# Two groups of DMA issues moved from ScalarE's queue to SyncE's in a fused attention and MoE kernel

## Chip, cores and metric

The kernel runs on one core of a Trainium2 chip. The metric is the device time of one launch in microseconds, from the first to the last instruction and what lies around it; lower is better. Times are medians of several runs.

## What is computed

The reference, cut to what matters:

```python
def _attn_ref(q, k, v, mem_k, mem_v):          # B=4, H=8, S=768, D=64
    chunk, left_ctx, right_ctx = (32, 16, 8)   # and 8 memory rows per head
    for c in range(S // chunk):
        k_full = concat([mem_k, k[l_start:r_end]]); v_full = concat([mem_v, v[l_start:r_end]])
        a = softmax(q_c @ k_full.T / sqrt(D))
        out[c] = a @ v_full
x = out.transpose(0, 2, 1, 3).reshape(3072, 512)
x = (sigmoid(x @ w_gate) * (x @ w_val)) @ w_out            # moe: 512 -> 1536 -> 512
h = x @ w_in; y = (h * sigmoid(1.702 * h)) @ w_out2        # moe2: 512 -> 2048 -> 512
```

All tensors are float32. The kernel keeps that precision by splitting each value into a high and a low fp32r part and multiplying three times.

## The kernel before

**Tokens.** The 3072 tokens are six blocks of 512 (`BLK`, `NB`). Attention works on 32 tiles of 96 tokens, each with all eight heads. Nine tiles go first; the other 23, called the late tiles here, are written by `attention_b` (L1001) in a fixed walk, one after the other, while TensorE works through the matmuls of moe for the first blocks (its input products L821 and L828, its output product L1020 in `gemm2`). The last two blocks' moe, and all of moe2, run later in a scheme of seven products in place of eight (L1318 and L1655); for these two blocks the attention's result goes through DRAM (`x_dram`).

**One late tile** in `attention` (L390): loads of q (12 DMAs into a buffer `f`), of k (16 to 20 DMAs into `raw` for a pair of tiles) and, for some, of mem_k; on VectorE the transposes `qt` (L532) and `kt` (L540), with copies of `kt` on ScalarE (L544); on TensorE one burst that holds the product with the values of the tile before (L704, `pv` from here on) and this tile's scores (L555); the softmax on VectorE, ScalarE and GpSimd; then `rest()` (L675), which loads the values, normalises, and transposes the probabilities. `rest()` calls `load_ctx("vn", ...)` (L405), which issues one DMA for v, one for mem_v and, at a sequence's first or last tile, one more. There is one buffer `vn`, so the loads for a tile can start when the tile before has had its `pv`, and have to land before its own. `evict()` (L720) copies the result out of PSUM: for the last two blocks on ScalarE into `qt` (L733), from where a DMA stores it to `x_dram`.

**What sets the order.** Every operation is a task with an engine, a planned duration, what it reads and writes, and for some a due time. `Schedule.run()` (L73) plays all tasks through in planned time and emits them, engine by engine, in the order in which they began there. On the chip every engine works its list in that order. A DMA's issue is a task of the engine that issues it. The helper `dma()` (L344) chooses it:

```python
q_ = nc.gpsimd if pool else nc.scalar if act else nc.sync
add("pool" if pool else "act" if act else "sp", dur, lambda: q_.dma_start(...), ...)
```

So ScalarE (ACT) issues what has `act=True`: before the change the late tiles' values and the stores to `x_dram`. It also issues the stores of moe's output to `y_dram` (L1044, with its own `nc.scalar.dma_start`). SyncE (SP) issues the loads of q, k and mem_k, the weights' loads, and everything of the later stages but a few.

**After the walk** `x_prep` (L1187) loads the four pieces of x of two blocks from `x_dram` on SP (L1194), forms their sums and differences (L1200) and high and low parts (L1178, L1182), and the seven products of L1318 begin. `produce1` (L1304) reloads weights from `wf_dram` for them.

Of the kernel before, what the change touches and what calls it, by code (L numbers as in the profile page):

```python
# [132 lines left out]
def c_dve(n, k=1):  # L133
    return k * 0.13 + n / 960.0


def c_act(n):
    return 0.13 + n / 1200.0
# [7 lines left out]
def kernel(  # L146
# [198 lines left out]
    def dma(dst, src, key, r=(), act=False, dur=0.45, pool=False):  # L345
        n = 8
        for d in src.shape:
            n *= d
        q_ = nc.gpsimd if pool else nc.scalar if act else nc.sync
        add("pool" if pool else "act" if act else "sp", dur, lambda: q_.dma_start(out=dst(), in_=src), r=list(r), w=[key], nbytes=n)  # L350
# [39 lines left out]
    def attention(t, bufs, banks, pe_path, extra=None, nth=0, last=False):  # L390
# [11 lines left out]
        def tadd(eng, dur, fn, r=(), w=(), more=0.0, **kw):  # L402
            add(eng, dur, fn, r=r, w=w, slack=SL + more, **kw)

        def load_ctx(name, src, mem, act=False):  # L405

            s0 = j * TQ - LEFT
            r0 = LEFT if j == 0 else 0
            r1 = TK - RIGHT if j == TPB - 1 else TK
            parts = [(r0, r1, src[b, :, s0 + r0 : s0 + r1, :]), (TK, P, mem[b])]  # L410
            if j == 0:
                parts.append((0, LEFT, src[b, :, 0:LEFT, :]))
            if j == TPB - 1:
                parts.append((r1, TK, src[b, :, S - RIGHT : S, :]))
            ks = []
            for i, (a, z, s) in enumerate(parts):
                ks.append((kk[name], i))
                dma(lambda a=a, z=z: T[name][a:z], s.rearrange("h s d -> s h d"), ks[-1], r=pre, act=act)
            for i in range(len(parts), 4):
                ks.append((kk[name], i))  # L420
            return ks
# [197 lines left out]
        def norm(eng, dst, rows_, keys):  # L619
            r = slice(*rows_)  # L620
            c = slice(*keys)
            n = rows_[1] - rows_[0]
            eng.tensor_tensor(  # L623
                out=dst, in0=e3()[r, :, c], in1=T["sm"][r].to_broadcast([n, H, keys[1] - keys[0]]), op=ALU.mult
            )

        if pe_path:

            def ev_norm(c):
                r = (c * CH, (c + 1) * CH)  # L630
                eng = nc.vector if en[c] == "dve" else nc.gpsimd
                norm(eng, T["pw"][r[0] : r[1], :, c * CH : c * CH + CTX], r, (0, CTX))

            def ev_norm_m():
                norm(nc.vector if en[0] == "dve" else nc.gpsimd, T["pw"][:, :, TK:P], (0, TQ), (CTX, KW))

            en = ["pool", "pool", "pool"] if t in (0, 2) else ["dve", "pool", "pool"]
            for c in range(NCK):
                tadd(en[c], 0.75 if en[c] == "dve" else 1.2, lambda c=c: ev_norm(c), r=ke + [kk["sm"]], w=[(kk["pw"], c)])
            tadd(en[0], 0.25 if en[0] == "dve" else 0.35, ev_norm_m, r=ke + [kk["sm"]], w=[(kk["pw"], 3)])  # L640

            def pe_pt(n):
                for h in range(H):
                    a, p = divmod(h, NP)
                    nc.tensor.transpose(  # L645
                        bt[a][:, p * TQ : p * TQ + n], T["pw"][:n, h, :], ident()[:n, :n]
                    )

            def ev_pt(a, n):
                src = bt[a][:, : NP * TQ].rearrange("p (h s) -> p h s", s=TQ)[:, :, :n]  # L650
                dst = T["pt"].rearrange("p (a h) s -> p a h s", a=2)[:, a, :, :n]
                nc.scalar.activation(dst, src, AF.Copy)

            def probs(n, more=()):
                bands = range(4) if n == TQ else (0, 3)
                r = [(kk["pw"], c) for c in bands] + [bufs.kid, *more]
                tadd("pe", 0.7 if n == TQ else 0.45, lambda: pe_pt(n), r=r, w=kbt, margin=mg)
                for a in range(2):
                    tadd("act", c_act(NP * n), lambda a=a: ev_pt(a, n), r=[kbt[a]], w=[(kk["pt"], a)])
        else:  # L660

            def ev_norm():
                norm(nc.gpsimd, T["pn"][0:L, :, 3 * CH - NM : 3 * CH], (0, L), (CTX, KW))
                norm(nc.gpsimd, T["pn"][L:TQ, :, CTX:KW], (L, TQ), (CTX, KW))

            PTB = ((0, 0, 0), (1, 0, 1), (2, 0, 2), (0, 1, 1), (1, 1, 2), (2, 1, 3), (0, 2, 3), (1, 2, 3))

            def ev_pt(part):
                for c, kb, r in PTB[2 * part : 2 * part + 2]:
                    nc.vector.transpose(  # L670
                        T["pt"][r * CH : (r + 1) * CH, :, c * CH : (c + 1) * CH],
                        T["pn"][c * CH : (c + 1) * CH, :, kb * CH : (kb + 1) * CH],
                    )

            def rest():  # L675
                load_ctx("vn", v, mem_v, True)
                tadd(
                    "pool",
                    0.95,
                    lambda: norm(nc.gpsimd, T["pn"][:, :, 0:CTX], (0, TQ), (0, CTX)),  # L680
                    r=ke + [kk["sm"]],
                    w=[(kk["pn"], 0)],
                )
                tadd("pool", 0.6, ev_norm, r=ke + [kk["sm"]], w=[(kk["pn"], 1)])
                for part in range(4):
                    tadd(
                        "dve",
                        0.88,
                        lambda part=part: ev_pt(part),
                        r=[(kk["pn"], 0), (kk["pn"], 1)],  # L690
                        w=[(kk["pt"], part)],
                    )
# [21 lines left out]
        def values(a, m, bk):  # L714
            if pe_path:
                return bk[:, : NP * TQ].rearrange("p (a s) -> p a s", a=NP)[:, :, a : a + m]
            src = both[:, :, NP * KW : NP * KW + NP // 2 * TQ]
            return src.rearrange("p o (a s) -> p o a s", s=TQ)[:, :, :, a : a + m]

        def evict(part=None, bk=bv, kpv=kpv):  # L720

            g = range(t * NCK, (t + 1) * NCK)
            for i, blk in enumerate(sorted({c // NCH for c in g})):
                if part not in (None, i):
                    continue
                cs = [c for c in g if c // NCH == blk]
                a = (cs[0] - g[0]) * CH
                m = len(cs) * CH
                x0 = cs[0] % NCH * CH
                xb = blk % 2  # L730
                if blk >= NB - 2:
                    src, dst = values(a, m, bk), T["qt"][:, :, :m].rearrange("p (o a) s -> p o a s", o=2)
                    tadd("act", c_act(NP * m), lambda d=dst, s=src: nc.scalar.activation(d, s, AF.Copy), r=kpv, w=[kk["qt"]])  # L733
                    o = (blk - NB + 2) * BLK + x0
                    dma(
                        lambda o=o, m=m: x_dram.rearrange("(a p) c -> p a c", p=P)[:, :, o : o + m],
                        T["qt"][:, :, :m],
                        ("xd", blk, t),
                        r=[kk["qt"]],
                        act=True,  # L740
                    )
                    continue
                due = None
                if t < NPRO and blk == 0:
                    due = clock[0] - STEP * (NPRO - 1 - t) - AHEAD
                elif t < NPE and blk <= 1 and SPREAD:

                    due = clock[0] + SPREAD * (t - NPRO + 1) / (NPE - NPRO)
                src = values(a, m, bk)
                wx = [("x", xb, c % NCH, e) for c in cs for e in range(2)]  # L750
                rx = kpv + (["x1"] if xb else [])

                def at(xs, x0=x0, m=m, xb=xb):
                    dst = xs[xb][:, :, x0 : x0 + m]
                    return dst if pe_path else dst.rearrange("p (o a) s -> p o a s", o=2)

                def ev_xh(src=src, at=at):
                    nc.scalar.activation(at(xhs), src, AF.Copy)

                def ev_xl(src=src, at=at):  # L760
                    nc.vector.tensor_tensor(out=at(xls), in0=src, in1=at(xhs).bitcast(F32), op=ALU.subtract)

                tadd("act", c_act(NP * m), ev_xh, r=rx, w=wx)
                tadd("dve", c_dve(NP * m), ev_xl, r=rx, w=wx, due=due)
# [1135 lines left out]
```

## Time and profile before

| | |
|---|---|
| median of 3 runs | 1128.76 us (1127.51 to 1131.07) |
| the profiled execution | 1130.38 us, span 1128.6 us |
| granted TensorE clock | 0.999 |
| TensorE matmul busy | 1116.4 us (99%) |
| VectorE, ScalarE, GpSimd busy | 842.4 us (75%), 589.6 us (52%), 161.6 us (14%) |
| DMA engines' mean busy share in the 40 slices | 0.2 to 0.9 |

The profile's page gives the busy time of each engine, in which the issuing of DMAs is not counted. The timeline lists what an engine did and, in brackets, how long it sat idle before and what ended that; a queue of an engine is written with a q (ACTq, SPq). The list of waits sums these idle times by pair of waiting and awaited line. The chain is the work that ended last, followed back from the end.

### The profile page before, as it was taken

The numbers are of one execution on the slowest core, as the hardware profiler recorded it, in microseconds if no ns is written. First come the engines' busy times: TensorE is split into PE (matmuls) and PEld (weight loads), VectorE is DVE, ScalarE is ACT, GpSimd is POOL, SyncE is SP. The second block draws the span as 40 slices with busy tenths as digits, with TensorE's granted clock in tenths as the row PEclk, the third lists the DMA queues.
The fourth block names the chain that finished last, engine by engine and source line by source line (L and its number), as shares of the span: only waits on it lengthen the run. The fifth ranks groups of instructions, "written<-read, shape, count | busy, mean of one in ns | idle before, by whom it ended". The sixth has DMA issues, their size and how long they took to land.

```text
span 1128.6 us, 19515 instructions
## 1 busy us (share of the span) xinstructions
PE 1116.4 (99%) x7190; PEld 933.7 (83%) x7190; DVE 842.4 (75%) x1440; ACT 589.6 (52%) x972; POOL 161.6 (14%) x209
## 2 busy tenths in 40 slices
PE   7999999999999999999999999999999999999998
PEld 6888899997888888888888888888888888888886
DVE  7989746776767788888887788869966369575365
ACT  5888632222222344676666777666455365354452
POOL 4332244122333113200001110000000000000000
PEclk9999999999999999999999999999999999999999
DMA  9676344335433555542556867868796666776526
GB/s 208 203 216 196 90 122 114 52 67 119 102 83 79 150 145 174 199 161 104 177 178 245 305 216 269 271 244 295 245 255 211 200 203 219 233 216 204 170 86 176
DMA packets 245903, 203.13 MB, mean 180 GB/s; under 512 B 170928, under 2 KB 191920, under 8 KB 245808
## 3 DMA queue, kind: packets, MB, share of 16 engines
q1 hardware_dynamic: 201560, 162.29, 48.9%
q0 software_dynamic: 6880, 24.12, 5.7%
q10 hardware_dynamic: 37368, 15.47, 5.0%
q8 instruction: 57, 0.93, 0.3%
q14 instruction: 38, 0.31, 0.1%
HBM read 151.49 MB, written 50.33 MB: 179 GB/s over the span
## 4 chain that ended last, share of the span: by engine, by line
PE 97%; DMA 1%; SPq 1%; ACT 0%; DVE 0%; issue 0%; ACTq 0%
PE bank L1318 30%; PE bank L1655 20%; PE bank L1020 18%; PE bank L821 15%; PE bank L828 8%; PE both L704 2%; PE both L555 2%; SPq L350 1%; PE bank L704 1%; PE bank L885 0%; DMA kn<-in_mem_k_dram 0%; PE bank L645 0%; DMA vn<-in_v_dram 0%; DMA w<-wo_dram 0%; PE both L645 0%
## 5 line engine op out<-in xcount | busy, mean ns | idle before, releaser
L1318 PE MATMUL bank<-sb_x,sb_r 128*128 128x512 f32 x1512 | 347.4, 389 | 0.0
L1318 PEld LDWEIGHTS bank<-sb_x,sb_r 128*128 128x128 f32 x1512 | 283.8, 188 | 58.9
L1655 PE MATMUL bank<-wq,w 128*128 128x512 f32 x756 | 178.0, 389 | 0.4 <-DMA w<-wo_dram 0.4
L1655 PEld LDWEIGHTS bank<-wq,w 128*128 128x128 f32 x756 | 141.8, 188 | 30.3 <-issue 0.8
L821 PE MATMUL bank<-xh,w 128*128 128x512 f32 (+1 forms) x464 | 159.6, 355 | 0.0
L821 PE MATMUL bank<-xl,w 128*128 128x512 f32 (+1 forms) x464 | 158.6, 353 | 0.0
L1334 DVE TENSOR_TENSOR sb_s<-bank,sb_s 128x512 f32<-128x512 f32 x108 | 74.4, 690 | 83.0 <-PE bank L1318 75.8
L828 PE MATMUL bank<-xh,w 128*128 128x512 f32 (+1 forms) x464 | 108.8, 356 | 0.0
L1020 PE MATMUL bank<-gh,wq 128*128 128x512 f32 (+1 forms) x448 | 98.7, 360 | 0.0
L821 PEld LDWEIGHTS bank<-xh,w 128*128 128x128 f32 x464 | 87.8, 189 | 12.6
L821 PEld LDWEIGHTS bank<-xl,w 128*128 128x128 f32 x464 | 87.8, 189 | 11.9
L1330 ACT ACTIVATE sb_s<-bank 128x512 f32<-128x512 f32 x108 | 64.8, 604 | 50.7 <-PE bank L1318 49.9
L828 PEld LDWEIGHTS bank<-xh,w 128*128 128x128 f32 x464 | 78.1, 189 | 12.4
L1020 PEld LDWEIGHTS bank<-gh,wq 128*128 128x128 f32 x448 | 76.4, 189 | 12.9
L670 DVE STREAM_TRANSPOSE pt<-raw 32x256 f32<-32x256 f32 x184 | 79.5, 432 | 4.7 <-POOL raw L623 2.1
L1626 DVE TENSOR_TENSOR wq<-xh_g,wq 128x1024 fp32r<-128x1024 f32 (+1 forms) x60 | 60.5, 1008 | 22.9 <-ACT wq L1623 22.5
L1623 ACT ACTIVATE wq<-xh_g 128x1024 fp32r<-128x1024 f32 (+1 forms) x60 | 53.3, 889 | 35.2 <-PE bank L1655 34.2
L853 ACT ACTIVATE gh<-sig 128x512 fp32r<-128x512 f32 (+1 forms) x58 | 32.3, 557 | 67.4 <-DVE sig L848 61.6
L623 POOL TENSOR_TENSOR raw<-e,sm 96x448 f32<-96x448 f32 (+2 forms) x69 | 41.0, 606 | 176.1 <-DVE sm L615 149.0
L1655 PE MATMUL bank<-wq,w_e 128*128 128x512 f32 x252 | 62.5, 389 | 0.0
L845 ACT ACTIVATE sig<-bank 128x512 f32<-128x512 f32 (+1 forms) x58 | 30.5, 526 | 55.5 <-PE bank L828 49.7
L1655 PEld LDWEIGHTS bank<-wq,w_e 128*128 128x128 f32 x252 | 47.3, 188 | 9.8
(215 smaller groups left out, 1646.1 us busy)
## 6 DMA issues: line engine op xcount, KB each, us to landing
sb_r<-wc_dram SPq DMA_DIRECT2D x133, 256.0 KB
w<-wo_dram SPq DMA_DIRECT2D x63, 512.0 KB
w_e<-wo_dram SPq DMA_DIRECT2D x21, 512.0 KB
wc_dram<-sb_r SPq DMA_DIRECT2D x15, 512.0 KB
wo_dram<-w POOLq DMA_DIRECT2D x14, 512.0 KB, 3.9
raw<-in_moe_w_out_dram SPq DMA_DIRECT2D x13, 512.0 KB
raw<-in_moe_w_in_dram SPq DMA_DIRECT2D x13, 512.0 KB
wf_dram<-f POOLq DMA_DIRECT2D x24, 256.0 KB, 2.9
```

The costliest lines, as they stand in the source:

```text
L623: eng.tensor_tensor(out=dst, in0=e3()[r, :, c], in1=T["sm"][r].to_broadcast([n, H, keys[1] - keys[0]]), op=ALU.mult)
L670: nc.vector.transpose(T["pt"][r * CH : (r + 1) * CH, :, c * CH : (c + 1) * CH], T["pn"][c * CH : (c + 1) * CH, :, kb * CH : (kb + 1) * CH],)
L704: nc.tensor.matmul((bk if to is None else to)[hp * D : (hp + 1) * D, o : o + q], T["vn"][:, 2 * p + hp, :], T["pt"][:, hp * NP + p, :q], s ...
L821: nc.tensor.matmul(bank[bk][:, :n], w[:, 0, ts[t]], x[xb][:, t, c0 : c0 + n], start=t == 0 and x is xhs, stop=False)
L828: nc.tensor.matmul(bank[bk][:, :n], w[:, 1, ts[t]], xhs[xb][:, t, c0 : c0 + n], start=False, stop=t == NK - 1)
L1020: nc.tensor.matmul(bank[into[m]][:, c0 : c0 + n], w[:, wi, m * P : (m + 1) * P], g[:, :n], start=f == 0 and j == 0 and c0 == 0, stop=f == ...
L1318: nc.tensor.matmul(bank[bk], w[:, o : o + P], xt[x, k][:, xl, :], start=first and k == 0 and wl == 0 and xl == 0, stop=k == 1 and wl == 1, ...
L1330: add("act", c_act(BLK), lambda: nc.scalar.activation(work[n], bank[bk], AF.Copy), r=[("bank", bk)], w=[n])
L1334: nc.vector.tensor_tensor(out=work[n], in0=bank[bk], in1=work[n], op=ALU.add)
L1623: nc.scalar.activation(quad[b_][:, c, 0, :], src(js), AF.Copy)
L1626: nc.vector.tensor_tensor(out=quad[b_][:, c, 1, :], in0=src(js), in1=quad[b_][:, c, 0, :].bitcast(F32), op=ALU.subtract)
L1655: nc.tensor.matmul(bank[bk], lhs, quad[b_][:, x, gl_, :], start=begin, stop=last and x == js[-1] and wl == 1, skip_group_check=not first,)
```

## The change

Two arguments change. `rest()` calls `load_ctx` without its last argument, so that the late tiles' loads of v and mem_v are tasks of SP. `evict()` calls `dma` without `act=True`, so that the stores to `x_dram` are tasks of SP too. Nothing else is edited. The stores of outputs (`y_dram` on ACT at L1044, `out_dram` in the last stage) stand as they stood.

```diff
             def rest():
-                load_ctx("vn", v, mem_v, True)
+                load_ctx("vn", v, mem_v)
...
                         T["qt"][:, :, :m],
                         ("xd", blk, t),
                         r=[kk["qt"]],
-                        act=True,
                     )
```

From L740 on a line of the changed kernel has a number one lower. The planner makes a new order out of this: 63 DMAs (28 of v, 23 of mem_v, 12 stores to `x_dram`) leave ACT's list, which goes from 1051 to 988 rows, and SP's goes from 442 to 518 rows, a row being a group of equal instructions.

**First place: ACT and SP around the eighth to tenth of the late tiles.** ACT's list of before, where a tile of the last blocks is copied out (L733) while outputs of moe are stored (L1040, L1044):

```order
282 L733 ACTIVATE qt<-both 128x384
283 L1040 ACTIVATE f_83<-bank_71 128x512
284 L350 DMA x_dram<-qt 128x4x96
285 L1044 DMA y_dram<-f_83 128x512
286 L350 DMA vn<-in_v_dram 112x8x64
287 L350 DMA vn<-in_mem_v_dram 8x8x64
288 L544 ACTIVATE kt<-f_82 128x12x8
289 L350 DMA vn<-in_v_dram 8x8x64
290 L853 ACTIVATE gh_87<-sig 128x512
291 L845 ACTIVATE sig<-bank_68 128x512
292 L1040 ACTIVATE f_83<-bank_73 128x512
293 L1044 DMA y_dram<-f_83 128x512
```

ACT's list of the change at the same place:

```order
265 L1039 ACTIVATE f_83<-bank_71 128x512
266 L733 ACTIVATE qt<-both 128x384
267 L1043 DMA y_dram<-f_83 128x512
268 L544 ACTIVATE kt<-f_82 128x12x8
269 L852 ACTIVATE gh_87<-sig 128x512
270 L844 ACTIVATE sig<-bank_68 128x512
271 L1039 ACTIVATE f_83<-bank_73 128x512
272 L1043 DMA y_dram<-f_83 128x512
```

SP's list of before there:

```order
111 L350 DMA f_81<-in_q_dram 32x4x32 x12
112 L350 DMA f_82<-in_q_dram 32x4x32 x12
113 L350 DMA raw_79<-in_k_dram 32x7x32 x16
114 L350 DMA f_81<-in_q_dram 32x4x32 x12
115 L350 DMA raw_78<-in_k_dram 32x7x32 x3
```

And SP's list of the change:

```order
129 L350 DMA vn<-in_v_dram 120x8x64
130 L350 DMA f_81<-in_q_dram 32x4x32 x12
131 L350 DMA vn<-in_mem_v_dram 8x8x64
132 L350 DMA f_82<-in_q_dram 32x4x32 x12
133 L350 DMA raw_79<-in_k_dram 32x7x32 x2
134 L350 DMA vn<-in_v_dram 112x8x64
135 L350 DMA vn<-in_mem_v_dram 8x8x64
136 L350 DMA x_dram<-qt 128x4x96
137 L350 DMA vn<-in_v_dram 8x8x64
138 L350 DMA raw_79<-in_k_dram 32x7x32 x14
139 L350 DMA f_81<-in_q_dram 32x4x32 x6
140 L350 DMA x_dram<-qt 128x4x96
```

The four DMAs between L733 and L853 have left ACT's list; they now stand in SP's, inside the groups of k and q loads.

**Second place: SP at the end of the walk, and TensorE's last `pv`.** SP's list of before:

```order
138 L350 DMA f_81<-in_q_dram 32x4x32 x12
139 L350 DMA f_82<-in_q_dram 32x4x32 x12
140 L1194 DMA xh_y<-x_dram 128x512 x2
141 L1304 DMA raw_78<-wf_dram 128x512 x2
142 L1304 DMA raw_79<-wf_dram 128x512 x2
143 L292 DMA raw_80<-in_moe_w_in_dram 128x4x128
144 L1194 DMA xh_y<-x_dram 128x512 x6
```

SP's list of the change:

```order
209 L350 DMA x_dram<-qt 128x4x96
210 L350 DMA vn<-in_v_dram 120x8x64
211 L350 DMA vn<-in_mem_v_dram 8x8x64
212 L350 DMA x_dram<-qt 128x4x96
213 L1303 DMA raw_78<-wf_dram 128x512
214 L350 DMA x_dram<-qt 128x4x96
215 L1303 DMA raw_78<-wf_dram 128x512
216 L1303 DMA raw_79<-wf_dram 128x512 x2
217 L292 DMA raw_80<-in_moe_w_in_dram 128x4x128
218 L1193 DMA xh_y<-x_dram 128x512 x6
```

TensorE's list of before around the last `pv`:

```order
1749 L1020 MATMUL bank_73<-gl_89,wq_745 128x512
1750 L704 MATMUL both<-pt,vn 64x96 x8
1751 L821 MATMUL bank_68<-xh_721,w_757 128x512
1752 L821 MATMUL bank_68<-xl_722,w_757 128x512
1753 L821 MATMUL bank_68<-xh_721,w_757 128x512
```

TensorE's list of the change, where the eight products of L820 and four of L827 stand ahead of it:

```order
1756 L820 MATMUL bank_68<-xh_721,w_757 128x512
1757 L820 MATMUL bank_68<-xl_722,w_757 128x512
1758 L827 MATMUL bank_68<-xh_721,w_757 128x512 x4
1759 L704 MATMUL both<-pt,vn 64x96 x8
1760 L820 MATMUL bank_69<-xh_721,w_758 128x512
```

The weights' loads from `wf_dram` now stand behind or between the last stores to `x_dram`, and the last `pv` is twelve matmuls later. TensorE's list has the same 2842 rows in both.

## Rows read from the trace of the kernel before

**Rows 1.** The page's busy times of the engines.

```profile
PE 1116.4 (99%) x7190; PEld 933.7 (83%) x7190; DVE 842.4 (75%) x1440; ACT 589.6 (52%) x972; POOL 161.6 (14%) x209
```

**Rows 2.** Waits of PE: waiting line, awaited line, us in total, times, longest.

```profile
PE bank L1020 <- ACT f L1040: 0.9, 1, 0.9
...
PE bank L1655 <- DMA w<-wo_dram: 0.4, 1, 0.4
```

**Rows 3.** Timeline of ACT, 273.5 to 282 us: start, duration, instruction, idle before it.

```profile
275.10 0.47 ACTq L1044 DMA_DIRECT2D y_dram<-f  x1
275.60 0.46 ACTq L350 DMA_DIRECT2D vn<-in_v_dram  x1
...
277.45 0.28 ACT L544 ACTIVATE kt<-f 128x96 f32<-128x96 f32 x1 [2.43 <-DMA y_dram<-f]
280.13 0.28 ACTq L350 DMA_DIRECT2D vn<-in_v_dram  x1
280.46 0.63 ACT L853 ACTIVATE gh<-sig 128x512 fp32r<-128x512 f32 x1 [2.72 <-DMA vn<-in_v_dram]
...
281.47 0.59 ACT L1040 ACTIVATE f<-bank 128x512 f32<-128x512 f32 x1
```

**Rows 4.** Chain of waits, 270 to 285 us: start, duration, what.

```profile
275.60 4.50 DMA vn<-in_v_dram
```

**Rows 5.** Timeline of PE, 281 to 283 us.

```profile
282.11 1.20 PE L1020 MATMUL bank<-gh,w 128*128 128x512 f32 x4 [0.86 <-ACT f L1040]
```

**Rows 6.** Line L350: count, duration min/median/max in ns, first and last start.

```profile
L350 SPq DMA_DIRECT2D f<-in_q_dram x276: 311/430/1766, 133.9 to 415.9; - x138
...
L350 ACTq DMA_DIRECT2D vn<-in_v_dram x28: 279/332/635, 142.5 to 450.7; - x28
...
L350 ACTq DMA_DIRECT2D x_dram<-qt x12: 377/420/1043, 274.6 to 459.6; - x12
```

**Rows 7.** Waits of SP's queue, 150 to 300 us.

```profile
SPq L350 <- DMA vn<-in_v_dram: 2.4, 2, 1.2
...
SPq L350 <- DVE qt L532: 0.2, 1, 0.2
```

**Rows 8.** Waits of SP's queue, 300 to 416 us.

```profile
SPq L350 <- DVE qt L532: 9.4, 4, 3.2
```

**Rows 9.** Timeline of SP, 240 to 275 us.

```profile
256.81 11.29 SPq L350 DMA_DIRECT2D f<-in_q_dram  x24
```

**Rows 10.** Timeline of DVE, 262 to 276 us.

```profile
265.59 0.56 DVE L532 STREAM_TRANSPOSE qt<-f 128x384 f32<-128x384 f32 x1
```

**Rows 11.** Timeline of PE, 270 to 276 us.

```profile
273.27 0.74 PE L555 MATMUL both<-kt,qt 64*32 64x64 f32 x48
```

**Rows 12.** Timeline of ACT, 380 to 402 us.

```profile
387.56 1.06 ACT L1040 ACTIVATE f<-bank 128x512 f32<-128x512 f32 x2
388.17 0.85 ACTq L1044 DMA_DIRECT2D y_dram<-f  x2
```

**Rows 13.** Timeline of PE, 384 to 392 us.

```profile
389.48 1.98 PE L1020 MATMUL bank<-gh,w 128*128 128x512 f32 x8
```

**Rows 14.** Timeline of SP, 372 to 486 us.

```profile
401.19 15.12 SPq L350 DMA_DIRECT2D f<-in_q_dram  x24
...
463.81 11.80 SPq L1194 DMA_DIRECT2D xh_y<-x_dram  x6
```

**Rows 15.** Chain of waits, 455 to 490 us.

```profile
460.96 1.81 PE bank L821 x8
462.77 0.91 PE bank L828 x4
...
482.72 7.48 PE bank L1318 x33
```

**Rows 16.** Timeline of ACT, 455 to 466 us.

```profile
459.64 0.39 ACTq L350 DMA_DIRECT2D x_dram<-qt  x1
```

**Rows 17.** Timeline of DVE, 455 to 486 us.

```profile
480.15 0.68 DVE L1182 TENSOR_TENSOR sb_x<-xl_y,sb_x 128x512 fp32r<-128x512 f32 x1
```

## The prediction

> **What bounds the kernel now.** I read the page's busy times first. TensorE's matmuls take 1116.4 of 1128.6 us [rows 1], so all that any change of queues can win is the 12.2 us in which TensorE has nothing to do. The list of TensorE's waits comes next, since it says which of this idle time hangs on another engine in the middle of the kernel: it is one stall of 0.9 us, in which L1020 waits for ScalarE's L1040, and one of 0.4 us, in which L1655 waits for a load of weights [rows 2]. The rest lies at the two ends of the program, where nothing is edited. The reader is to see that a gain from this change is bounded by the first stall, with the second at most 1.3 us. That is far below 0.3% (3.4 us), about what a measurement of this kernel can tell from no change.
>
> The third view is the timeline at that stall. TensorE resumes L1020 at 282.11 us after 0.86 us of idleness [rows 5]. It waited for the copy at 281.47, which stood on ScalarE behind two pauses of 2.43 and 2.72 us, and in the second of them behind a third piece of `vn` that was issued at 280.13 [rows 3]. The chain shows why so late: the first piece, issued at 275.60, took 4.50 us, and the third piece goes out as it lands [rows 4]. So an issue on ScalarE's queue held up arithmetic that TensorE needed. This is the thing that the change takes away.
>
> The fourth view is SyncE's queue, which gets the DMAs. From 150 to 300 us its waits are seven groups of which the largest is 2.4 us and the smallest 0.2, together 5.3 us [rows 7]; it issues nearly all the time, 24 q loads in 11.29 us, 0.47 us each [rows 9]. From 300 to 416 it has more room, 9.4 us of waiting for q's buffers alone [rows 8]. So the queue that is added to is the fuller one, and the question is if it stays ahead of TensorE.
>
> **The change part by part.** *Removed from ScalarE:* 28 loads of v at 0.33 us, 23 of mem_v, which I take at the same, and 12 stores at 0.42 [rows 6], some 22 us of issues and the pauses beside them. ScalarE is busy for 52% [rows 1], so this is worth only what TensorE waited for: **−0.86 us** [rows 5]. After the change ScalarE's list there holds one y store between L733 and L853. If it should wait as long as ScalarE did in the pauses above, TensorE would get its 0.86 us back; I count the gain as whole.
>
> *The y stores that stay on ScalarE.* A DMA's issue can wait for an earlier DMA's landing, as [rows 3, 4] show, and which one it is changes with the new order. The tightest place is the next block, where two copies of L1040 end at 388.62, two y stores follow [rows 12], and TensorE takes the banks at 389.48 [rows 13]: 0.86 us to spare. If a store waited for 4.50 us ahead of a copy, as long as the landing in [rows 4], TensorE would lose 3.6 us; if it stands behind the copies, as now, nothing. I take **0.2 us**, near the lower end, because in the trace the two stores there went out without a pause.
>
> *Added to SyncE.* 63 issues at 0.47 us are 29.6 us over a stretch of 282 us. Cover for them is SyncE's waiting, and how far ahead of its use a load is. I follow the place where this is thinnest. The q of the tenth late tile is the first half of the 24 loads of [rows 9] and is issued by 262.5 us. Its transpose ran at 265.59 and ended at 266.15 [rows 10]; the scores that read it began at 273.27 [rows 11]. That is 7.1 us to spare. In the new list 16 moved loads stand ahead of this q: 16 x 0.47 = 7.5 us later. The 5.3 us of waiting up to 300 us [rows 7] could absorb part, which leaves 2.2 us; against that SyncE now has to wait itself for the `pv` that frees `vn`, with the next q and k loads queued behind. A tile's 20 q and k loads leave 12.6 − 20 x 0.47 = 3.2 us of the planner's spacing of 12.6 us (L388), so two such waits would cost 6.4 us and make the lag 13.9. The stall on TensorE is lag less 7.1 us: from 0 to 6.8 us. I take the lag without either, 7.5 us, so **0.4 us**. From 300 to 416 us some nine tiles bring 18 loads and the stores about 7 more, 11.8 us, against 9.4 us of waiting [rows 8]; where SyncE waits for a q buffer its loads go out as early as the buffer allows, so I count the 2.4 us left there as covered.
>
> *Moved at the end of the walk.* The last `pv` stands behind twelve more matmuls, 1.81 + 0.91 = 2.72 us [rows 15]. The store of its tile to `x_dram`, at 459.64 before [rows 16], and SyncE's loads of x, at 463.81 [rows 14], follow it and come that much later. SyncE's reloads of weights now stand behind the last store, but SyncE was idle from 416 us, where its q loads ended, but for a few loads [rows 14], so there they cost nothing unless the x loads wait behind them. The first product L1318 starts at 482.72 [rows 15]; the latest of its operands that VectorE made before it was ready at 480.83 [rows 17]. So 1.9 us is cover, and 2.72 − 1.9 = **0.8 us** is left. The ends are 0, if VectorE fills the delay with weight work that it would else do later, and 5.1, if nothing is absorbed and five reloads (2.4 us) stand ahead of the x loads too. TensorE's list is otherwise the same length, so no matmul time is added; after 490 us nothing is edited.
>
> **Sum:** −0.86 + 0.2 + 0.4 + 0.8 = +0.54 us. The profiled execution took 1130.38 us, 1.62 above the median of the runs shown; against it the sum gives 1130.9, and against the median 1128.76 it gives **1129.3 us**.
>
> **A rule against the row.** [Rows 9] show 0.47 us per issue on a queue that hardly waits, and the sum goes by that. The Trainium skill's page DMA: Bandwidth & Descriptors, section Issuing engines are not separate DMA queues, says that DMAs started by different engines run on the same 16 DMA engines, and that starting them from several saves only issue time, usually small beside the transfer. By that rule the move would cost nothing on SyncE and the sum would be −0.86 + 0.2 + 0.8 = +0.14 us, 1128.9. In this trace the issue time is not small: 29.6 us in all, on a queue with 5.3 us of waiting in its fullest 150 us [rows 7].
>
> **The rivals.**
>
> *SyncE falls behind.* One mechanism, at the q loads of the ninth to eleventh late tiles. For it: the queue has 5.3 us of free time in 150 us [rows 7] and is given 16 issues before the tenth tile's q. Against it: the 7.1 us between transpose and scores. It decides from a lag of 7.1 us; at the upper end of 13.9 the stall is 6.8 us: 1128.76 − 0.86 + 0.2 + 0.8 + 6.8 = **1135.7 us**, slower. The Trainium skill's page Perfetto Trace Analysis, section DMA Optimizations, advises to spread DMAs over the engines that can start them where an engine looks full of issues; that speaks for this rival, as the change does the opposite, and no run here shows yet which of the two it is.
>
> *The x loads come late for L1318.* For it: the 2.72 us, and the reloads ahead of the x loads. Against it: 19 us between the first x load and L1318 [rows 14, 15]. It decides where VectorE cannot make good more than the 1.9 us. With 5.1 in place of 0.8 us: 1129.3 + 4.3 = **1133.6 us**.
>
> *The stall goes and nothing takes its place.* For it: 7.1 us of spare for q and 19 us for x. Then 1128.76 − 0.86 = **1127.9 us**, and with the stall at L1655 gone too, 1127.5.
>
> *The change does not do what it says.* Its words name outputs' stores on ScalarE, and no line of the diff moves one: the y stores were there before [rows 12]. So this part is worth nothing, and the forecast holds without it.
>
> **How the numbers follow.** Chances: forecast 0.67, no stall in its place 0.12, SyncE behind 0.10, x late 0.08, and 0.03 for a gain that no row shows. Faster by over 0.3% is only the last, 0.03. Slower by over 0.3% (above 1132.1 us) are SyncE behind and x late, with 0.01 of the forecast's own tail: 0.19. The same: 0.78. The range reaches from 1127.0 (the best case, 1127.5, less half a microsecond for the scatter of the runs) to 1133.8, which takes in the late x loads and leaves out SyncE at its upper end and the unseen gain, 0.13.
>
> **What the profile after would show.** If the steps are right: no wait of L1020 on L1040 near 281 us; ScalarE without pauses put down to `vn` or `x_dram`; SyncE with hardly a wait up to 300 us, its q loads of the tenth late tile some 5 to 8 us later; the last q loads a few us after 416 us; and TensorE's only new stall near 483 us, at the first L1318, of about 0.8 us. A wait of L555 on a q transpose would show SyncE behind; a wait at L1318 of over 3 us would show the x loads late. A new wait of L704 for `vn` or of L1020 for a y store would make the sum wrong in its second term. A time below 1127 us would show that I missed time of TensorE's that the list of waits does not count.

## The result, and the profile after

The changed kernel takes **1134.65 us** (median of 6 runs, 1132.70 to 1136.84) against 1128.74 before (6 runs, 1127.51 to 1131.07): a ratio of 1.0051, 95% interval 1.0036 to 1.0066. It is slower by 5.9 us. The forecast was 1129.3, the range 1127.0 to 1133.8.

The page's busy times of the changed kernel, which answer to [rows 1]:

```profile
PE 1120.6 (99%) x7190; PEld 936.7 (83%) x7190; DVE 841.7 (74%) x1440; ACT 588.5 (52%) x972; POOL 160.5 (14%) x209
```

The profiled execution has a span of 1135.1 us, 6.5 more than the one before. TensorE has the same 7190 matmuls and is busy 4.2 us longer, so its idle time does not tell all. TensorE's waits from 134 to 520 us, which answer to [rows 2] (waiting line, awaited line, us in total, times, longest):

```profile
PE both L704 <- DMA vn<-in_mem_v_dram: 4.8, 2, 2.9
PE both L704 <- issue: 0.4, 1, 0.4
```

The stall of L1020 (now L1019) on ScalarE's copy is gone, as forecast. In its place two `pv`'s wait for their values. TensorE's timeline at both places (start, duration, instruction, idle before it):

```profile
296.36 0.39 PE L820 MATMUL bank<-xl,w 128*128 128x512 f32 x1
298.68 1.32 PE L704 MATMUL both<-pt,vn 128*64 128x96 f32 x16 [1.94 <-DMA vn<-in_mem_v_dram]
...
403.25 0.39 PE L820 MATMUL bank<-xl,w 128*128 128x512 f32 x1
406.54 0.88 PE L704 MATMUL both<-pt,vn 128*64 128x96 f32 x16 [2.90 <-DMA vn<-in_mem_v_dram]
...
409.76 0.63 PE L820 MATMUL bank<-xh,w 128*128 128x512 f32 x1
410.19 0.63 PE L820 MATMUL bank<-xl,w 128*128 128x512 f32 x1
```

The last two rows show a second price. The same matmul that took 0.39 us before the stall takes 0.63 behind it, and they begin 0.43 us apart. TensorE's stretches (start and end, length, busy time, count, granted clock, DMA share, GB/s):

```profile
275.00:295.00 20.00, 20.00 (x145) 1.00 0.51 123
295.00:300.00 5.00, 3.06 (x30) 0.90 0.42 83
300.00:305.00 5.00, 5.00 (x64) 0.76 0.41 109
...
405.00:410.00 5.00, 3.46 (x69) 0.82 0.44 88
410.00:415.00 5.00, 5.00 (x20) 0.84 0.39 69
415.00:420.00 5.00, 5.00 (x24) 1.00 0.50 103
```

The granted clock is 1.00 up to each stall. In stretches of 1 us it is 0.50 from 299 to 302 us and from 409 to 411, the lower of the two levels (1.2 in place of 2.4 GHz), and 1.00 again by 303 and by 412:

```profile
299.00:300.00 1.00, 1.00 (x20) 0.50 0.29 56
409.00:410.00 1.00, 1.00 (x4) 0.50 0.18 25
```

The loss can be followed by the scores' bursts (L555) that both kernels run in the same order. In the profiled executions the burst at 273.27 us [rows 11] began at 272.05 after the change, 1.22 earlier, a difference that was there by the burst at 63.09 us (61.87 after), ahead of the late tiles, where nothing is edited. The first L1318 (now L1317) began at 482.72 before [rows 15] and at 489.38 after, 6.66 later. So between the two points the change lost 1.22 + 6.66 = 7.9 us; in this TensorE's idleness is 1.94 + 2.90 + 0.42 = 5.26, less the 0.86 that it no longer loses at 281 us, or 4.4. The other 3.5 us are the slower clock; what the granted clock lacks to 1.00 in stretches of 1 us adds up to 3.4.

**Why the values were late.** SyncE's timeline of the changed kernel ahead of the second stall, and ScalarE's at the same time:

```profile
384.23 6.77 SPq L350 DMA_DIRECT2D raw<-in_k_dram  x4
391.55 11.06 SPq L350 DMA_DIRECT2D f<-in_q_dram  x22
402.70 0.89 SPq L350 DMA_DIRECT2D vn<-in_v_dram  x2
403.69 0.38 SPq L350 DMA_DIRECT2D x_dram<-qt  x1
404.12 0.41 SPq L350 DMA_DIRECT2D vn<-in_mem_v_dram  x1
```

```profile
388.15 0.33 ACTq L1043 DMA_DIRECT2D y_dram<-f  x1
388.48 0.57 ACT L1039 ACTIVATE f<-bank 128x512 f32<-128x512 f32 x1
389.08 0.33 ACTq L1043 DMA_DIRECT2D y_dram<-f  x1
```

Four k loads, some 1.8 us of issues, stretch over 6.8: SyncE stands still. Then 22 q loads go out, and only behind them the values. The chain of waits over this stretch (start, duration, what) says what SyncE stood still for:

```profile
389.08 2.45 DMA y_dram<-f
391.53 0.02 issue
391.55 0.84 SPq L350
...
404.12 2.28 DMA vn<-in_mem_v_dram
406.40 0.14 issue
406.54 0.88 PE both L704 x16
```

It waited for a store of moe's output, which ScalarE had yet to issue, to land. Nothing in the data ties a k or q load to that store. Ahead of the first stall it was the same, with smaller pauses. SyncE's waits from 265 to 296 us begin with

```profile
SPq L350 <- DMA y_dram<-f: 3.4, 2, 2.8
```

and its timeline has 12 q loads stretched to 8.73 us, and the values of the tile behind them and the k and q loads that follow:

```profile
268.85 8.73 SPq L350 DMA_DIRECT2D f<-in_q_dram  x12
...
295.36 0.89 SPq L350 DMA_DIRECT2D vn<-in_v_dram  x2
296.30 0.33 SPq L350 DMA_DIRECT2D vn<-in_mem_v_dram  x1
```

SyncE's waits from 134 to 420 us add it up:

```profile
SPq L350 <- DMA y_dram<-f: 10.7, 5, 5.1
SPq L350 <- PE both L704: 1.5, 2, 1.3
```

In [rows 7] the same kind of wait stood first, for `vn`, then issued by ScalarE. From 134 to 420 us the kernel before had less than half as much of it:

```profile
SPq L350 <- DMA vn<-in_v_dram: 3.9, 4, 1.2
```

### The profile page after: what moved, and what is told of

It is laid out like the page before. It is cut to its first block, busy times and chain, and to the rows that moved or that the text cites. A ratio compares the mean times of both kernels' runs of the same rounds, so it can differ in the third digit from the quotient of the medians.

```text
span 1135.1 us, 19530 instructions
## 1 busy us (share of the span) xinstructions
PE 1120.6 (99%) x7190; PEld 936.7 (83%) x7190; DVE 841.7 (74%) x1440; ACT 588.5 (52%) x972; POOL 160.5 (14%) x209
## 4 chain that ended last, share of the span: by engine, by line
PE 88%; SPq 5%; DMA 3%; DVE 2%; issue 1%; ACT 0%; DVEq 0%; ACTq 0%
PE bank L1317 30%; PE bank L1654 20%; PE bank L1019 15%; PE bank L820 12%; PE bank L827 6%; SPq L350 5%; PE both L704 1%; PE both L555 1%; DMA f<-in_q_dram 1%; DVE pt L670 1%; DMA y_dram<-f 1%; PE bank L704 1%; PE bank L884 0%; PE bank L645 0%; DMA vn<-in_mem_v_dram 0%
## 5 line engine op out<-in xcount | busy, mean ns | idle before, releaser
L1317 PE MATMUL bank<-sb_x,sb_r 128*128 128x512 f32 x1512 | 347.3, 389 | 0.0
L1317 PEld LDWEIGHTS bank<-sb_x,sb_r 128*128 128x128 f32 x1512 | 283.8, 188 | 58.9
L820 PE MATMUL bank<-xh,w 128*128 128x512 f32 (+1 forms) x464 | 159.9, 356 | 0.0
L820 PE MATMUL bank<-xl,w 128*128 128x512 f32 (+1 forms) x464 | 159.0, 354 | 0.0
L827 PE MATMUL bank<-xh,w 128*128 128x512 f32 (+1 forms) x464 | 110.3, 360 | 0.0
L1019 PE MATMUL bank<-gh,wq 128*128 128x512 f32 (+1 forms) x448 | 99.0, 361 | 0.0
L820 PEld LDWEIGHTS bank<-xh,w 128*128 128x128 f32 x464 | 88.2, 190 | 12.9
L820 PEld LDWEIGHTS bank<-xl,w 128*128 128x128 f32 x464 | 88.1, 190 | 12.1
L827 PEld LDWEIGHTS bank<-xh,w 128*128 128x128 f32 x464 | 78.9, 191 | 12.6 <-issue 0.2
L1019 PEld LDWEIGHTS bank<-gh,wq 128*128 128x128 f32 x448 | 76.4, 189 | 13.1
L623 POOL TENSOR_TENSOR raw<-e,sm 96x448 f32<-96x448 f32 (+2 forms) x69 | 38.2, 564 | 181.9 <-DVE sm L615 142.2
L844 ACT ACTIVATE sig<-bank 128x512 f32<-128x512 f32 (+1 forms) x58 | 30.5, 526 | 64.0 <-PE bank L827 63.5
```

What stands on the lines that cost most here:

```text
L623: eng.tensor_tensor(out=dst, in0=e3()[r, :, c], in1=T["sm"][r].to_broadcast([n, H, keys[1] - keys[0]]), op=ALU.mult)
L820: nc.tensor.matmul(bank[bk][:, :n], w[:, 0, ts[t]], x[xb][:, t, c0 : c0 + n], start=t == 0 and x is xhs, stop=False)
L827: nc.tensor.matmul(bank[bk][:, :n], w[:, 1, ts[t]], xhs[xb][:, t, c0 : c0 + n], start=False, stop=t == NK - 1)
L1019: nc.tensor.matmul(bank[into[m]][:, c0 : c0 + n], w[:, wi, m * P : (m + 1) * P], g[:, :n], start=f == 0 and j == 0 and c0 == 0, stop=f == ...
L1317: nc.tensor.matmul(bank[bk], w[:, o : o + P], xt[x, k][:, xl, :], start=first and k == 0 and wl == 0 and xl == 0, stop=k == 1 and wl == 1, ...
```

## The experiments

The planner lays out a new order after every edit, so two of these kernels differ in more than the edited lines; where that bears on a reading, it is said. Three theories were tried. A, called F in the last expectations: SyncE's queue is too full with 63 more issues. B: SyncE's loads wait for ScalarE's y stores to land, and the values stand behind these loads; B2 is A and B together, issues and pauses both taking SyncE's time. C: the x stores in SyncE's list hold up what stands behind them. All runs are compared with the kernel before on the same chip.

**Which of the two moves costs.** `e1_values_only` leaves the x stores on ScalarE (this diff and those below are against the changed kernel):

```diff
                         ("xd", blk, t),
                         r=[kk["qt"]],
+                        act=True,
                     )
```

> Only the loads of v and mem_v move to SyncE; the x_dram stores stay on ScalarE. In the changed kernel's trace TensorE loses its time at two pv's (L704) that wait for vn, 1.94 us at 298 and 2.90 at 406, each with a stretch of lower granted clock behind it, because vn's loads stand behind q loads in SyncE's list. Theory A (the queue is simply too full: 63 more issues of 0.45 us): 51 of the 63 issues are still there, so most of the loss stays, about 51/63 of 5.9 = +4.8 us, 1133.5 (1132 to 1135). Theory B (SyncE is held up by waits for ScalarE's y stores to land, 10.7 us in 5 times, and the vn loads stand behind these): the y stores are still on ScalarE, so the loss stays too, 1132 to 1135. Theory C (the stores of x in SyncE's list hold up what stands behind them): no loss, 1127.5 to 1129.

Measured: 1136.18 us, ratio 1.0058 (1.0044 to 1.0073). `e2_x_only` moves only the stores:

```diff
-                load_ctx("vn", v, mem_v)
+                load_ctx("vn", v, mem_v, True)
```

> Only the 12 stores to x_dram move to SyncE; values stay on ScalarE. Theory A (too full): 12 of 63 issues, so +1.1 us at most, 1128.7 to 1130. Theory B (waits for y stores, with vn behind them): no vn on SyncE, so no L704 wait, 1127.5 to 1129.5; the stall of L1020 on L1040 near 281 may stay, since vn's third piece still stands on ScalarE. Theory C (the x stores hold up SyncE): the loss stays, 1132 to 1135.

Measured: 1129.01 us, ratio 1.0008 (0.9996 to 1.0021). The whole loss belongs to the values; theory C falls. e1 lies 1.2 us above the range that both A and B gave, so it does not tell these two apart.

**Taking y off ScalarE.** `e3_y_gpsimd` is the changed kernel with one engine changed:

```diff
             def store(m=m, st=st):
-                nc.scalar.dma_start(out=y_dram[...], in_=st[:, :n])
+                nc.gpsimd.dma_start(out=y_dram[...], in_=st[:, :n])
-            add("act", 0.1, store, ...)
+            add("pool", 1.0, store, ...)
```

> The changed kernel with the 24 y_dram stores issued by GpSimd in place of ScalarE; SyncE's list stays as it is but for one q group. Theory A (too full): SyncE has the same issues, so the waits of L704 for vn and the time stay, 1133 to 1136. Theory B (coupling): SyncE's waits for y (10.7 us in 5 times) go from its list of waits, vn's loads go out 3 to 6 us earlier at 295 and 402, both waits of L704 go, and the time is 1128 to 1130. Between the two (1130 to 1133) if only one of the two stalls goes.

Measured: 1130.94 us, ratio 1.0018 (1.0007 to 1.0029), 3.7 us below the changed kernel, and the two intervals do not overlap. TensorE's waits from 134 to 486 us, and SyncE's timeline at the place shown above:

```profile
PE both L704 <- ACT sig L844: 0.7, 1, 0.7
```

```profile
381.33 1.83 SPq L350 DMA_DIRECT2D raw<-in_k_dram  x4
383.20 11.93 SPq L350 DMA_DIRECT2D f<-in_q_dram  x22
395.22 0.89 SPq L350 DMA_DIRECT2D vn<-in_v_dram  x2
```

The same four k loads take 1.83 us in place of 6.77, and the values go out 7.5 us earlier, at 395.22. SyncE's waits no longer name y, and both stalls are gone. The time is 0.9 us above theory B's range. What the edit does by itself was measured on the kernel before, `e7_before_y_gpsimd`, with the same diff:

> The kernel before with the y_dram stores issued by GpSimd: what that costs or gives by itself, for the reading of e3_y_gpsimd (1130.94, 1.0018). If it is free: 1127.9 to 1129.5, and the 2 us that e3_y_gpsimd is above the kernel before belong to the moved loads. If GpSimd's issues of 0.6 to 1 us hold up its normalising: 1130 to 1132, and then the moved loads cost nothing once y is off the two shared queues.

Measured: 1129.03 us, ratio 1.0007 (0.9995 to 1.0019): free. So of the 5.9 us y's stores on ScalarE cost 3.7, and they cost it only together with the moved loads.

**All on SyncE.** `e6_y_sync` puts y's stores on SyncE as well:

```diff
-                nc.scalar.dma_start(out=y_dram[...], in_=st[:, :n])
+                nc.sync.dma_start(out=y_dram[...], in_=st[:, :n])
-            add("act", 0.1, store, ...)
+            add("sp", 0.45, store, ...)
```

> The changed kernel with the 24 y_dram stores on SyncE as well. Theory A (too full): 24 more issues of 0.45 us, 10.8 us more of lag, 11 of them before the first stall, so longer waits of L704 for vn or of L555 for q, 1138 to 1146. Theory B (coupling between two queues): all of these DMAs are in one list, so a load no longer waits for a store that another engine has yet to issue; the waits put down to y shrink below 4 us, and the time is not above the changed kernel's, 1129 to 1134.6.

Measured: 1138.39 us, ratio 1.0078 (1.0060 to 1.0095), in time at the lower end of A and a miss for B. The waits are those of neither. SyncE waits no more for y to land, as B said, and the long waits for `vn` or q that A named are not there either: TensorE waits mostly for arithmetic of VectorE and ScalarE. Its waits from 134 to 486 us have these first and last:

```profile
PE bank L820 <- DVE sig L847: 1.7, 1, 1.7
...
PE both L704 <- DMA vn<-in_mem_v_dram: 0.6, 2, 0.4
```

SyncE's waits from 134 to 420 us have a new first row, and ScalarE, whose copies need the buffers that y's stores empty, waits longer for these stores to land (2.6 us in the changed kernel):

```profile
SPq L1043 <- ACT f L1039: 3.6, 2, 3.3
```

```profile
ACT f L1039 <- DMA y_dram<-f: 9.2, 3, 3.5
```

A y store in SyncE's list waits for ScalarE's copy, and the loads behind it wait too. So this run does not tell 24 issues from such waits, and the last experiment was made for that.

**Fewer issues on SyncE.** `e8_mem_v_back` gives the loads of mem_v back to ScalarE, `e10_mem_v_gpsimd` gives them to GpSimd, `e11_mem_v_y_gpsimd` gives GpSimd y's stores too, by e3's diff. The edit of e8:

```diff
-                dma(lambda a=a, z=z: T[name][a:z], ..., r=pre, act=act)
+                dma(lambda a=a, z=z: T[name][a:z], ..., r=pre, act=act and z == P)
-                load_ctx("vn", v, mem_v)
+                load_ctx("vn", v, mem_v, True)
```

In e10 and e11 the new line of `dma` ends `r=pre, pool=act and z == P`.

> The changed kernel with the 23 loads of mem_v back on ScalarE: SyncE gets 40 issues in place of 63. Theory B2: 23 x 0.45 = 10.4 us of SyncE's time come free, as much as the waits for y take, so the L704 waits for v shrink to under 2 us in total, 1129 to 1132. Rival (only the coupling of the two queues matters, not how much SyncE issues): SyncE still waits for y, and now also for mem_v on ScalarE and the other way round, so it stays at 1133 to 1137.

> The changed kernel with the 23 loads of mem_v issued by GpSimd: SyncE gets 40 issues in place of 63, and unlike in e8_mem_v_back ScalarE gets none, so the only DMAs of ScalarE in the walk are y's stores, as in the changed kernel. Theory F (SyncE's time: its issues fill it): 10.4 us come free, the time is 1129 to 1131.5. Theory B (coupling: SyncE's loads wait for y's stores to land, at the wrong moments, however many it issues): its waits for y stay at 5 us or more, a wait of L704 or L555 of over 1 us stays in the walk, 1131.5 to 1136.

> As e10_mem_v_gpsimd, with y's stores on GpSimd too, so that ScalarE issues no DMA in the walk. Both theories: no wait for y on SyncE. If e3_y_gpsimd's 1.9 us above e7_before_y_gpsimd are SyncE's fullness, they go, 1128 to 1130; if GpSimd's longer list of issues holds up its normalising, 1130 to 1134.

Measured: e8 1135.57 us, ratio 1.0054 (1.0038 to 1.0069); e10 1132.74, 1.0034 (1.0021 to 1.0047); e11 1130.32, 1.0012 (1.0003 to 1.0021). In e8 23 issues fewer helped nothing that can be measured; its rival held. SyncE's waits show two kinds of another engine's DMA there:

```profile
SPq L350 <- DMA vn<-in_mem_v_dram: 5.5, 6, 1.8
SPq L350 <- DMA y_dram<-f: 3.0, 5, 1.1
```

e10's time and its `pv` that waits 3.4 us for v are as theory B said, while SyncE's waits for y, 3.6 us, stay below the 5 that it named. e10 lies 1.9 us below the changed kernel, but the intervals overlap, so it is open if fewer issues give anything while the waits for y stay. Taking y away from e10, as e11 does, gives 2.4 us back; their intervals touch at 1.0021. e11's time is just inside the range given for a GpSimd that holds up its normalising, but its trace does not show that: TensorE's longest wait there is 1.0 us, for v.

**Giving back only the tiles that waited.** Both stalls are at tiles that begin a sequence. `e9_first_tile_back` puts their six DMAs back on ScalarE:

```diff
-                load_ctx("vn", v, mem_v)
+                load_ctx("vn", v, mem_v, j == 0)
```

> The changed kernel with the values of the two late tiles that begin a sequence (three pieces each, 6 DMAs) back on ScalarE; these are the two tiles whose pv waited. Theory B2: the loss is in these two waits and the clock behind them, so 1128.5 to 1131, with no wait of L704 over 1 us. Rival (the whole queue is late and another tile would wait next): a wait of the same size appears at another pv or at L555, 1132 to 1135.

Measured: 1136.84 us, ratio 1.0065 (1.0046 to 1.0083). My expectation was wrong. Its rival held in kind, though the time lies 1.8 us above the rival's range too: TensorE's waits from 134 to 486 us begin with

```profile
PE both L555 <- DVE qt L532: 4.8, 2, 4.4
PE both L704 <- DMA vn<-in_mem_v_dram: 1.8, 1, 1.8
```

The lateness only moved: now it is q's transposes that came late for the scores. SyncE waits 5.6 us for y and 4.6 us for the values that ScalarE issues again, so the run does not tell a late queue from more such waits.

**Values ahead of q.** `e4_values_first` gives the values' loads 8 us of slack in the planner (`slack=8.0`, handed from `rest()` through `load_ctx` and `dma` to `add`), and `e12_first_y_gpsimd` is the same with e3's diff.

> The changed kernel, but a late tile's loads of values have 8 us of slack in the planner, so that they stand some rows earlier in SyncE's list, most of them ahead of the q group they stood in or behind. So far: moving only the x stores costs nothing (1129.0), moving only the values costs everything (1136.2), and taking y's stores off ScalarE gives 3.7 of the 5.9 us back. Theory B2 (SyncE has too little time for its own issues plus the 10.7 us of waits for y, and what is late in the end is whatever stands behind the q loads): the two waits of L704 for vn at 298 and 406 shrink to under 1 us each, SyncE's waits for y stay at 8 to 11 us, and the lateness goes to q, which has some us to spare: 1129.5 to 1132. Rival (the queue itself is over-full, so any order is late): waits move from L704 to L555 or the transposes of q, 1133 to 1137.

> e4_values_first (1143.1) with y's stores on GpSimd. Theory F (SyncE full, so with values ahead q and k are late in any case): 1137 to 1143. Theory B (the waits for y are what makes things late): 1129 to 1133.

Measured: e4 1143.09 us, ratio 1.0124 (1.0103 to 1.0144); e12 1139.08, 1.0089 (1.0076 to 1.0102). e4 lies above both of its ranges. e12 lies in theory F's and outside B's, but for another reason than F gave: no wait of TensorE's from 134 to 520 us names q, k or `vn`, and the two largest are for arithmetic (2.7 us for L847, 2.1 for L844). They are no clean test of the order of values and q: the planner moved arithmetic as well, and before 270 us both kernels have the same new waits of TensorE, of which the first two are, in e4:

```profile
PE bank L820 <- ACT sig L844: 1.1, 2, 0.5
PE bank L820 <- DVE sig L847: 1.1, 2, 0.8
```

What the pair does tell: with y on GpSimd 4.0 us come back, much as from the changed kernel to e3, and the wait of 2.4 us for `vn` that e4 still has is gone.

**More issues without coupling.** `e13_two_mem_v` is e3 with mem_v of the late tiles loaded in two halves:

```diff
+            if t >= NPE and name == "vn":
+                parts[1:] = [(TK, TK + 4, mem[b][:, :4]), (TK + 4, P, mem[b][:, 4:])]
```

> e3_y_gpsimd (1130.94; y's stores on GpSimd, SyncE waits for no other engine's DMA) with each late tile's load of mem_v cut into two halves: 23 more issues on SyncE, 10.4 us of its time, with the same bytes and no new dependency. Theory F (how much SyncE issues decides once the coupling is gone): values or q come late again, a wait of L704 or L555 of over 1 us in the walk, 1133 to 1139, as e6_y_sync (24 more issues, 1138.4) suggests. Theory B alone (only the coupling costs): 1130 to 1132, no such wait; then what made e6_y_sync slow was the order of its list and not the number of issues.

Measured: 1128.96 us, ratio 1.0004 (0.9988 to 1.0020). TensorE's waits from 134 to 520 us are two:

```profile
PE both L706 <- DVE sm L614: 0.6, 1, 0.6
PE both L706 <- DMA vn<-in_mem_v_dram: 0.3, 1, 0.3
```

The first of them is at 449 us and the second at 425. SyncE's timeline at the place of the first stall, and the `pv` there in e3 and in e13:

```profile
289.51 4.14 SPq L350 DMA_DIRECT2D f<-in_q_dram  x8
293.76 0.90 SPq L350 DMA_DIRECT2D vn<-in_v_dram  x2
```

```profile
297.01 0.88 PE L704 MATMUL both<-pt,vn 128*64 128x96 f32 x16
```

```profile
298.89 0.88 PE L706 MATMUL both<-pt,vn 128*64 128x96 f32 x16
```

SyncE issues 86 DMAs more here than in the kernel before, 23 more than after the change. The values go out at 293.76 us, 2.1 later than in e3 (291.64), but the planner also made TensorE's `pv` 1.9 later, so they are 5.1 us ahead of it in place of 5.4. In the changed kernel they went out at 295.36, 3.3 us ahead of a `pv` that had waited 1.94. At the second place the planner put 12 q loads ahead of the values in place of e3's 22. So e13 is not e3 with 23 issues put in between. What it shows is that a list with 86 more issues can be laid out at no cost that can be measured: theories A and F fall for the amounts tried, in the orders that the planner made. Together with e3 and e7 it leaves the pauses for y as what overran the time to spare.

## Why the prediction was wrong

*The gain.* The stall at 281 us went, −0.86 us, as the first term said.

*"The y stores that stay on ScalarE", 0.2 us.* I looked for the price on ScalarE, and there it was nothing: ScalarE waited 2.6 us for y's landing, and TensorE lost none of it. The reader can see the mistake in [rows 3, 4]: an issue waited for another DMA's landing, and I followed this only along the queue on which I had seen it. The same waits lay on SyncE's side, 10.7 us in five times. Taking y off ScalarE gives 3.7 us (e3), 4.0 (e12) and 2.4 (e11), and the same edit on the kernel before gives nothing (e7). This is shown, for e3 and e12 with intervals that do not overlap. By the prediction's last paragraph a wait of L704 for `vn` would make the sum wrong in this term; it did, though the price came due in the next.

*"Added to SyncE", 0.4 us.* This is the step that failed: the term made SyncE late by the time of the issues alone, put SyncE's waits for DMAs of ScalarE at nothing, and looked only where q has the least to spare. The lag was about right there: the q of the tile that it followed was all issued by 268.4 us, 5.9 later than before, and q's 7.1 us of spare held. The one wait that it named, for the `pv` that frees `vn`, came to 1.5 us in two times; the waits for y came to 10.7. And what was late was `vn` itself, which I had not followed as a load in its own right: in the new list it stands behind one or two q groups, 12 or 22 loads, and after a pause of SyncE ahead of them it lands too late for its `pv`. In the profiled execution the loss, with the gain of 0.86 added, is 7.9 + 0.86 = 8.8 us. Of this 4.84 is idleness at the two `pv`'s and 3.5 the clock behind them, which is 8.3 us for this term; the rest is 0.42 at the last `pv`, taken up below. The forecast had priced stalls as idleness alone. Behind 300 us I had counted the lag as covered, and the last q load a few us late: it began at 429.4 us in place of 415.9. But it did so at 429.8 in e13, which lost nothing that can be measured.

*The issues themselves.* I had argued that 29.6 us of issues are not small. With y off the two shared queues a list with 23 further issues costs nothing that can be measured (e13). The rule of the Trainium skill's page DMA: Bandwidth & Descriptors, section Issuing engines are not separate DMA queues, that only issue time is at stake and is usually small, agrees with e13; for the change as it is it would have given 1128.9, no nearer than my sum, since it does not speak of one engine's issue waiting for another's DMA.

*"Moved at the end of the walk", 0.8 us.* No wait of L1317 appears at its start. The last `pv` was idle for 0.42 us, which the profile puts down to "issue" and no run explains; the term was 0.42 us at most.

*The rivals.* "SyncE falls behind" came nearest, 1135.7 with a chance of 0.10. It had the place wrong (q's transposes in place of `vn`) and half the cause: SyncE did fall behind, but what e3, e7 and e13 point to is the pauses for y, not the number of issues. What it would take was named in the last paragraph, a wait of L704 for `vn`; it was given no price.

What stays open: why e3 is at 1.0018 and e13, with more issues, at 1.0004; the intervals overlap, and e3's trace shows no stall of that size. Also how much of e6's loss SyncE's waits for the copies cost, how much ScalarE's waits for the buffers, and how much the other order. Fewer issues with y left on ScalarE gave 1.9 us that the intervals do not part from nothing (e10). And no run broke the coupling while y stayed on ScalarE.

## What to carry to other kernels

Before moving DMAs to another engine's queue, look in that queue's waits for DMAs which other engines issue: each is a place where the queue may stop for something that its own data do not need, and everything moved there stops with it. Follow every moved load to its own consumer, with what newly stands ahead of it, and not only the loads that it delays. A full queue that runs late may cost nothing (e13), while in this kernel the pauses ahead of the loads did, 3.4 us in two times at the first place and one of 5.1 us at the second.

## What was not expected of the hardware

A load on SyncE's queue stood still for 5.1 us until a store that ScalarE issued later had landed, with no tie in the data. No view shows what ties the two, so it may lie in the program as well as in the chip. And behind idle stretches of 1.9 and 2.9 us TensorE, busy without a break for over 100 us before the first of them, got a lower clock: 0.50 from 299 to 302 us and from 409 to 411, with matmuls of 0.63 us in place of 0.39. That added 3.5 us to 4.8 us of idleness. The stall of 0.86 us in the kernel before [rows 5] has no such stretch behind it in that trace, whose mean clock is 0.999.
